# Planner costs, single-engine routing steps, late bias tables and numbered one-hot rows in an attention and expert kernel

## The chip, the cores and the metric

The kernel runs on one core of one Trainium2 chip. The metric is device time in microseconds for one execution; it was taken three times. PE is the matrix engine (TensorE), DVE the vector engine, ACT the scalar engine, POOL is GpSimd, and SP issues most of the DMAs. Each engine executes its own queue in order and waits at an instruction until what that instruction needs is there.

## The reference

Two parts follow each other. Windowed attention for 8 batches and 8 heads over 576 positions with 64 values each (window 128, a linear bias per head), then a layer of 8 experts on the 4608 rows of 512 values. Each token takes the expert with the largest logit, or keeps that of the token before it where a local gate says so.

```python
scores = np.where(mask, scale * q @ k.T + bias, -1e9)   # mask: 0 <= rel < 128
attn = softmax(scores); x = attn @ v                    # rows of 8 heads * 64
for b in range(B):
    for s in range(S):
        fresh_e = argmax(logits[b, s])
        e = fresh_e if s == 0 or local_gate[b, s] < 0.5 else prev_e
        prev_e = e
        p = softmax(logits[b, s])
        out[b, s] = p[e] * (relu(x[b, s] @ w1[e]) @ w2[e])
```

## The kernel before, in words

**Attention** runs over 32 pairs of heads (8 batches of 4 pairs). A pair is a chain of small operations, named by a letter. S (PE) makes nine pieces of scores in PSUM, four banks of them. D (DVE) scales a piece, adds the bias table and takes the row minimum (`scs<-sc`, with a short read of the minimum, `mn`). E (ACT) is the exponential, with its sum; B (DVE) is that sum for two of the pieces, where DVE makes it. A and R (DVE) make the reciprocal of the sums (`r`). P (POOL or DVE) multiplies the piece by it (`cut<-cut,r`). U (PE) transposes (`pt<-ident,cut`), C (ACT or DVE) copies the result out of PSUM (`pts<-pt`), M (PE) multiplies by the values (`xa<-pts,cut`), X (ACT or DVE) copies that out (`xT<-xa`), and T (DVE) transposes 32x32 blocks for the store (`T<-xT`).

The bias tables of a pair are six DVE or POOL operations on `rel` (which lies in the tile `qx`); their results lie in `slopes` and `qx`. Pair 0's six go to DVE; the other 18 may be taken by either engine and wait for nothing.

**Routing** of a batch, `tokens` and `route`, follows when its four pairs are through: logits (PE), then some 35 short steps on DVE and POOL that find the expert of each token, its gate value and its place in that expert's list. `route` gives a one-hot matrix `ro_all` (row within a block) per batch. For the first three experts, which the kernel serves first ("own" visits of 256, 384 and 384 rows), it also builds `cw` and adds the token numbers into a table `tbl`; `early` turns that table into indices, and `gathers` fetches the rows with indirect DMAs on POOL (`kr<-xd,xidx`).

**The planner** (`plan`, `Op`, `steps`) decides the order of all this while the kernel is built: it keeps a clock for each engine, charges every instruction the duration that `cost` gives, and picks the operation that can start first; among equals the smaller due time wins (`DUE`, in pairs). `COPY` and `SHARE` say for each operation which engines may take it, and `SLOWER` is what DVE is charged on top before it takes a copy that ACT could do. A step of a generator in `steps` is one such operation; where a `yield` stands, the next step begins, and its word says on which engine. `BY` is added to the due time from step to step. The instructions of the planned engines keep the planned order; the expert stage behind it is put in between by the framework where it finds room.

**Experts.** `Fixed.run` works through a visit: for each of eight slices of the hidden layer `h<-qx,cut` (PE), relu and a split into two parts (ACT `hh`, DVE `hl`), then `y<-cut,hh`. The weights come in raw (`wraw`) and each half chunk is split by ACT (`CAST cut<-wraw`) and DVE (`TENSOR_TENSOR cut<-wraw,cut`). Rows of a visit are turned by DVE (`xtr<-kr`), ACT (`qx<-xtr`) and DVE (`qx<-xtr,qx`). A tick in between advances `routing`: the routing of batch 7, then `rank_tables` and `fill_table`, which build the lists of the remaining visits from `ro_all` and one-hot columns (`hot`).

## Time and profile before

| what | value |
| --- | --- |
| time, median of 3 (lowest to highest) | 670.52 us (670.30 to 670.69) |
| the profiled execution | 671.84 us, of which the span of the profile is 670.1 us |
| PE busy | 644.6 us (96%) |
| DVE busy | 512.4 us (76%) |
| ACT busy | 412.9 us (62%) |
| POOL busy | 370.6 us (55%) |
| mean granted clock of PE | 0.985 |

Attention ends on PE at about 223.5 us of the span, the experts take the rest. A busy time counts a stretch in which at least one instruction of the engine was under way. A row of the timeline gives start, duration, engine, line, operation, out<-in, shape and count; in brackets stands the idle time of the engine ahead of it and what ended it. Line 226 is the planner's recording helper, so most of attention has this line; the tile names tell the operations apart.

### The profile page before, as it was taken

To read this page: it belongs to the slowest core of one execution; us is meant where nothing else is said; L and a number is where in the kernel's file an instruction comes from. 1 tells how busy PE (TensorE), PEld (TensorE's weight loads), DVE (VectorE), ACT (ScalarE), POOL (GpSimd) and SP (SyncE) were. 2 spreads that over 40 slices of the span, in tenths; PEclk is the share of its full clock that TensorE was granted. 3 is DMA by queue.
4 is the path that set the end of the run, shared out by engine and by line. 5 is a ranking of instruction groups with operands and counts; after the bars stand their busy time and mean duration, and the time that the engine had idled before them with its cause. 6 is when DMAs were issued, how large, how long until landed. Compare 5 with 4: busy or idle time off the path is not lost. (4 is left out here: it accounts for less than half of the span.)

```text
span 670.1 us, 17317 instructions
## 1 busy us (share of the span) xinstructions
PE 644.6 (96%) x5913; PEld 515.0 (77%) x5913; DVE 512.4 (76%) x1882; ACT 412.9 (62%) x1148; POOL 370.6 (55%) x567
## 2 busy tenths in 40 slices
PE   6999999999998989999999999999999999999995
PEld 3676766766665877899888889889988988888663
DVE  7899999999998799896454995675676576566883
ACT  4999999999887563344343554553555455455651
POOL 6456466455856776277651847557476466526411
PEclk7999999999998999999999999999999999999998
DMA  9863965853933674465632576666566574447640
GB/s 284 290 212 120 266 188 150 265 168 114 303 110 108 200 237 159 137 209 159 192 92 95 181 258 181 206 207 203 162 216 207 160 237 118 148 134 226 216 158 21
DMA packets 61964, 122.22 MB, mean 182 GB/s; under 512 B 9687, under 2 KB 28759, under 8 KB 61874
## 3 DMA queue, kind: packets, MB, share of 16 engines
q1 hardware_dynamic: 52322, 101.27, 47.9%
q0 software_dynamic: 9120, 19.24, 9.5%
q8 instruction: 47, 0.77, 0.5%
q10 hardware_dynamic: 432, 0.59, 0.3%
q14 instruction: 43, 0.35, 0.2%
HBM read 102.08 MB, written 19.04 MB: 181 GB/s over the span
## 5 line engine op out<-in xcount | busy, mean ns | idle before, releaser
L242 POOL DMA_INDIRECT kr<-xd,xidx x141 | 158.1, 1122 | 57.8 <-issue 41.6
L312 DVE TENSOR_TENSOR cut<-wraw,cut 128x512 fp32r<-128x512 f32 x232 | 151.4, 687 | 31.1 <-ACT cut L310 30.0
L310 ACT CAST cut<-wraw 128x512 fp32r<-128x512 f32 x222 | 127.0, 618 | 42.1 <-PE y L1333 40.2
L1331 PE MATMUL h<-qx,cut 128*128 128x384 f32 (+7 forms) x408 | 130.4, 320 | 1.7 <-ACT qx L253 1.7
L1332 PE MATMUL h<-qx,cut 128*128 128x384 f32 (+7 forms) x408 | 130.2, 319 | 0.1
L1333 PE MATMUL h<-qx,cut 128*128 128x384 f32 (+7 forms) x408 | 130.2, 319 | 0.0
L226 ACT ACTIVATE cut<-scs,mn 128x192 f32<-128x192 f32 (+2 forms) x288 | 121.1, 436 | 14.4 <-DVE mn L226 13.6
L1331 PE MATMUL y<-cut,hh 128*128 128x512 f32 (+2 forms) x288 | 115.4, 401 | 2.7 <-DVE hh L1421 2.7
L226 POOL TENSOR_SCALAR cut<-cut,r 128x192 f32<-128x192 f32 (+2 forms) x205 | 84.7, 429 | 58.6 <-DVE r L226 17.1
L1318 POOL DMA_INDIRECT out<-y,sidx x41 | 43.9, 1072 | 132.2 <-ACT y L1340 69.6
L1333 PE MATMUL y<-cut,hl 128*128 128x512 f32 (+2 forms) x288 | 114.2, 396 | 0.1
L1332 PE MATMUL y<-cut,hh 128*128 128x512 f32 (+2 forms) x288 | 113.6, 394 | 0.0
L1424 DVE SCALAR_TENSOR_TENSOR hl<-h,hh 128x384 fp32r<-128x384 f32 (+4 forms) x104 | 51.2, 495 | 64.2 <-ACT hh L1423 63.9
L1423 ACT ACTIVATE hh<-h 128x384 fp32r<-128x384 f32 (+4 forms) x98 | 43.7, 446 | 84.5 <-PE h L1333 81.2
L226 PE MATMUL sc<-kr,qx 64*64 64x192 f32 (+2 forms) x1152 | 83.0, 332 | 6.3 <-DVE mn L226 6.3
L1331 PEld LDWEIGHTS h<-qx,cut 128*128 128x128 f32 x408 | 77.4, 190 | 7.4 <-ACT qx L253 2.2
L1332 PEld LDWEIGHTS h<-qx,cut 128*128 128x128 f32 x408 | 77.7, 190 | 5.0 <-DVE qx L255 0.4
L1333 PEld LDWEIGHTS h<-qx,cut 128*128 128x128 f32 x408 | 77.7, 190 | 1.3
L226 PE MATMUL xa<-pts,cut 64*64 64x64 f32 (+1 forms) x1280 | 72.1, 254 | 2.5 <-ACT xT L226 2.2
L1331 PEld LDWEIGHTS y<-cut,hh 128*128 128x128 f32 (+2 forms) x288 | 53.5, 186 | 21.1 <-DVE hl L1424 3.3
L226 PEld LDWEIGHTS xa<-pts,cut 64*64 64x64 f32 (+1 forms) x1280 | 48.1, 135 | 23.9 <-issue 8.7
L226 PE MATMUL pt<-ident,cut 128*128 128x128 f32 x384 | 64.1, 289 | 0.7 <-POOL cut L226 0.7
(237 smaller groups left out, 1043.0 us busy)
## 6 DMA issues: line engine op xcount, KB each, us to landing
wraw<-w SPq DMA_DIRECT2D x120, 512.0 KB
kr<-kT SPq DMA_DIRECT2D x31, 288.0 KB
qx<-qT SPq DMA_DIRECT2D x30, 288.0 KB
cut<-v SPq DMA_DIRECT2D x8, 1024.0 KB
xd<-T SPq DMA_DIRECT2D x8, 640.0 KB
xd<-T SPq DMA_DIRECT2D x8, 512.0 KB
kr<-xd,xidx POOLq DMA_INDIRECT x141, 3.7
v<-v SPq DMA_DIRECT2D x16, 128.0 KB
```

The source lines that it names most:

```text
L226: ins = getattr(self.engine, name)(*args, **kw)
L242: queued(nc.gpsimd.indirect_dma_start(out=r, out_offset=None, in_=src[0:n, :], in_offset=bass.IndirectOffsetOnAxis(ap=col, axis=0), bounds ...
L310: scalar.copy(c[:, 0, f], raw[:, f])
L312: vector.tensor_tensor(c[:, 1, f], raw[:, f], c[:, 0, f], ALU.subtract)
L1318: ins = nc.gpsimd.indirect_dma_start(out=out[:, :], out_offset=bass.IndirectOffsetOnAxis(ap=col, axis=0), in_=y, in_offset=None, bounds_ch ...
L1331: nc.tensor.matmul(o, ah, bh, start=start, stop=False)
L1332: nc.tensor.matmul(o, ah, bl, start=False, stop=False)
L1333: nc.tensor.matmul(o, al, bh, start=False, stop=stop)
L1423: now.act.activation(hh, hp[:, :w], AF.Relu)
L1424: nc.vector.scalar_tensor_tensor(hl, hp[:, :w], 0.0, hh, ALU.max, ALU.subtract)
```

## The change

Seven edits, in one step:

- the planner's durations for some DVE operations are raised, `SLOWER` goes from 34 to 120 and `BY` from 0.113 to 0.172, and `DUE`, `COPY` and `SHARE` hold other values;
- `route` is cut into more steps, each with instructions of one engine; the exponential is issued later, and `rex` is multiplied ahead of `ohs`;
- the 18 tables of pairs 1 to 3 wait each for a D of the pair before;
- `ro_all` is multiplied by the token numbers `val` (POOL; DVE for batch 7), which `hv` did before for `cw`, and `hot` for each column;
- `hot` is one `tensor_tensor` over five columns in place of five `tensor_scalar`;
- `val` already tells three batches apart, so `enter_steps` adds the offset of a batch only from batch 3 on;
- that addition is a POOL step of its own.

```diff
 DUE = {
-    "A0": 0.47, "A1": -0.1,
+    "A0": -1.48, "A1": -2.34,
...
-SCS, SLOWER, SWITCH, STORE, BY = 8, 34, 0, 10000, 0.113
-COPY = {"C0": "aaea", "C1": "aaea", "C2": "aeae", "X0": "eeee", "X1": "aeae"}
-SHARE = ["fpff", "pfpf", "ffff", "fpff", "ffff", "fpff", "ffff", "fffp", "fffp"]
+SCS, SLOWER, SWITCH, STORE, BY = 8, 120, 0, 10000, 0.172
+COPY = {"C0": "aeee", "C1": "aaea", "C2": "aeae", "X0": "eeae", "X1": "aeee"}
+SHARE = ["fppf", "pfpf", "ffff", "fpff", "ffff", "fpfp", "ffff", "fffd", "fffp"]
...
         if name == "tensor_tensor_reduce":
-            return 75 + 1.04 * n
+            return 80 + 1.04 * n
         if name == "tensor_scalar" and 64 <= n <= 192 and args[1].dtype == F32:
-            return 60 + 0.88 * n
+            return 90 + 1.1 * n
+        if name == "tensor_scalar" and n <= 32:
+            return 110
         if name == "tensor_reduce":
-            return 45 + (src if src >= 64 else 1.3 * src)
+            return 66 + 1.05 * src if src >= 64 else 45 + 1.3 * src
...
             dve.tensor_tensor(a5, l8, mb, ALU.is_equal)
+            for _ in step:
+                yield "pool"
             apart.tensor_tensor(a5, a5, kp, ALU.mult)
             apart.tensor_tensor(ex, l8, mb, ALU.subtract)
...
             dve.tensor_reduce(c, a5, AX.X, ALU.max)
-            act.activation(ex, ex, AF.Exp)
...
             dve.tensor_tensor_scan(run_, kT, kT, 0.0, ALU.max, ALU.max)
+            for _ in step:
+                yield "act"
+            act.activation(ex, ex, AF.Exp)
...
+            for _ in step:
+                yield "pool"
+            apart.tensor_tensor(ex, ex, OH, ALU.mult)
             apart.tensor_tensor(ohs, ohs, cn, ALU.add)
-            apart.tensor_tensor(ex, ex, OH, ALU.mult)
...
             dve.tensor_tensor(RO, rep32.unsqueeze(1).broadcast_to([P, NT, P]), rf.unsqueeze(2).broadcast_to([P, NT, P]), ALU.is_equal)
+            for _ in step:
+                yield "pool"
+            apart.tensor_tensor(RO, RO, val[:, b % 3].unsqueeze(2).broadcast_to([P, NT, P]), ALU.mult)
...
-            pool.tensor_tensor(hv, OH[:, :, 0:NS], val[:, 0].unsqueeze(2).broadcast_to([P, NT, NS]), ALU.mult)
-            pool.tensor_tensor(cw, hv.unsqueeze(3).broadcast_to([P, NT, NS, 4 * KS]),
+            yield "pool"
+            pool.tensor_tensor(cw, OH[:, :, 0:NS].unsqueeze(3).broadcast_to([P, NT, NS, 4 * KS]),
                                    kh.unsqueeze(2).broadcast_to([P, NT, NS, 4 * KS]), ALU.mult)
...
+        def enter_steps(table, ps, b):
+            if b < 3:
+                dve.tensor_tensor(table, table, ps, ALU.add)
+                return
+            z = tp.tile([P, P], F32, name="tz")[:, :table.shape[1]]
+            dve.tensor_scalar(z, ps, 0.0, float(S * (b - b % 3)), ALU.is_gt, ALU.mult)
+            dve.tensor_tensor(table, table, ps, ALU.add)
+            yield "pool"
+            pool.tensor_tensor(table, table, z, ALU.add)
...
+            if 0 < n < 4:
+                for j in range(6):
+                    def table(e, j=j):
+                        bias_table(n, j, dve if e == "dve" else pool)
+
+                    tables[n, j] = Op("pool dve", n - 0.9 + 0.1 * j, table, [ops["D", j, n - 1]])
...
-            for t in range(NT):
-                nc.vector.tensor_scalar(fo[b][:, t], io128, fc[:, b * NT + t:b * NT + t + 1], val[:, b % 3, t:t + 1], ALU.is_equal, ALU.mult)
+            nc.vector.tensor_tensor(fo[b], io128.unsqueeze(1).broadcast_to([P, NT, NSB]),
+                                    fc[:, b * NT:b * NT + NT].unsqueeze(2).broadcast_to([P, NT, NSB]), ALU.is_equal)
```

What this does to the order of the instructions is shown at three places; a row is line, operation, out<-in and shape, and xN is a count. Lines of the changed kernel are two higher in the helpers. The first place is DVE's queue at the start, first as it was and then as it is; the rows on `qx` and `slopes` are bias tables, the rows named ISA are D and the reading of its minimum.

```order
L226 TENSOR_SCALAR qx<-qx 64x192 x2
L226 TENSOR_SCALAR slopes<-qx 128x192 x2
L226 TENSOR_SCALAR slopes<-qx 64x192 x2
L226 TENSOR_SCALAR qx<-qx 64x192 x2
L226 TENSOR_SCALAR slopes<-qx 128x192
L226 TENSOR_SCALAR qx<-qx 64x192 x3
L226 TENSOR_SCALAR slopes<-qx 128x192 x2
L226 TENSOR_SCALAR qx<-qx 64x192 x3
L226 ISA scs,mn<-sc,slopes 128x192
L226 ISA mn 128x1
L226 ISA scs,mn<-sc,slopes 128x192
```

```order
L228 TENSOR_SCALAR qx<-qx 64x192 x2
L228 ISA scs,mn<-sc,slopes 128x192
L228 ISA mn 128x1
L228 ISA scs,mn<-sc,slopes 128x192
L228 ISA mn 128x1
L228 ISA scs,mn<-sc,slopes 128x192
L228 ISA mn 128x1
L228 ISA scs,mn<-sc,slopes 128x192
L228 ISA mn 128x1
L228 TENSOR_SCALAR slopes<-qx 64x192
L228 ISA scs,mn<-sc,slopes 128x192
L228 ISA mn 128x1
```

Of the 18 tables of pairs 1 to 3, 15 stood on DVE ahead of the first D; now none does. In all, DVE makes 11 tables in place of 21, and POOL 13 in place of 3.

The second place is POOL's queue at the routing of batch 6, the last one that the planner sees. `ra` and `rex` are steps of it, the DMA rows are gathers of expert rows, and `cut<-cut,r` are P operations.

```order
L242 DMA kr<-xd,xidx_116 128x128
L226 TENSOR_SCALAR cut<-cut,r 128x192
L242 DMA kr<-xd,xidx_116 128x128
L226 TENSOR_SCALAR cut<-cut,r 128x128
L242 DMA kr<-xd,xidx_116 128x128
L226 TENSOR_TENSOR ra<-ra,kp 128x40
L226 TENSOR_TENSOR rex<-L,rm 128x40
L226 TENSOR_SCALAR cut<-cut,r 128x192 x2
L226 TENSOR_SCALAR cut<-cut,r 128x64
```

```order
L228 TENSOR_TENSOR ra<-ra,kp 128x40
L228 TENSOR_TENSOR rex<-L,rm 128x40
L244 DMA kr<-xd,xidx_116 128x128
L228 TENSOR_SCALAR rse<-rse 128x5
L244 DMA kr<-xd,xidx_116 128x128 x2
L228 TENSOR_TENSOR rex<-rex,oh_all 128x40
L228 TENSOR_TENSOR ohs<-ohs,cn 128x8
L228 CAST rrf<-ri 128x5
L228 TENSOR_TENSOR ro_all<-ro_all,val 128x640
L244 DMA kr<-xd,xidx_116 128x128 x9
```

The three gathers ahead of `ra` now stand behind it, no P operation is left behind this routing, and nine further gathers stand behind the multiplication of `ro_all`.

The third place is DVE's queue where attention ends (`T<-xT` is the T operation, and the last of them stands here). The row with 512 columns on `cut<-wraw,cut` is DVE's half of splitting a half chunk of weights; `ed`, `ti` and `bi` belong to `early`, `rc`, `k` and `kT` to the routing of batch 6.

```order
L226 TENSOR_TENSOR ro_all<-rep_91,rrf 128x640
L226 TENSOR_TENSOR cut<-wraw,cut 128x512
L226 STREAM_TRANSPOSE T<-xT 128x10x32
L226 STREAM_TRANSPOSE T<-xT 128x8x32
L226 TENSOR_TENSOR cut<-wraw,cut 128x512
L1424 SCALAR_TENSOR_TENSOR hl<-h,hh 128x256 x2
L312 TENSOR_TENSOR cut<-wraw,cut 128x512
L226 COPY L<-pk 128x36
L226 TENSOR_REDUCE L<-pk 128x9
L312 TENSOR_TENSOR cut<-wraw,cut 128x512
```

```order
L228 TENSOR_REDUCE rc<-ra 128x5
L228 STREAM_TRANSPOSE T<-xT 128x8x32
L228 TENSOR_TENSOR cut<-wraw,cut 128x512
L228 TENSOR_SCALAR ti<-tbl 128x32
L228 TENSOR_SCALAR bi<-ti 128x32
L228 TENSOR_TENSOR k_109<-rc,rf 128x5
L228 SCALAR_TENSOR_TENSOR fi<-bi,ti 128x32
L228 STREAM_TRANSPOSE kT<-k_109 128x32
L228 TENSOR_SCALAR xidx_116<-fi,roff 128x32
L228 SCALAR_TENSOR_TENSOR krun<-kT 128x32
L228 TENSOR_TENSOR cut<-wraw,cut 128x512
L228 TENSOR_TENSOR fi<-tbl,msel 128x32
```

Before, the routing of batch 6 and `early` were done ahead of the last T, and one split stood between it and the first `hl` of an expert. Now 28 short steps of them, the building of `ro_all` for batch 6 and six splits stand behind the last T and ahead of the copy of batch 7's logits. On PE, 22 products of the first visit (`h<-qx,xT`) stood among the last products of attention; now all of them stand behind it. The first five loads of raw weights, which stood on SP behind the stores of batch 5, now stand among the loads of batch 2.

## Rows read from the trace of the kernel before

**Rows 1.** busy time by stretch; the first line names the columns.

```profile
core 0: us, PE busy (x) PEld busy (x) DVE busy (x) ACT busy (x) POOL busy (x), PEclk, DMA share, GB/s
7.80:18.10 10.30, 7.40 (x64) 4.92 (x65) 8.40 (x53) 7.21 (x28) 4.70 (x26) 0.50 1.07 330
20.00:200.00 180.00, 176.19 (x3089) 123.22 (x3087) 170.65 (x1027) 166.64 (x601) 100.04 (x269) 1.00 0.64 195
205.80:209.20 3.40, 3.27 (x24) 2.04 (x24) 3.29 (x14) 2.83 (x11) 1.89 (x4) 0.50 0.20 76
225.00:250.00 25.00, 22.96 (x141) 19.32 (x141) 24.36 (x79) 15.60 (x34) 18.80 (x16) 1.00 0.79 245
250.00:640.00 390.00, 388.48 (x2134) 333.89 (x2134) 266.32 (x574) 191.92 (x398) 217.79 (x196) 1.00 0.57 179
```

**Rows 2.** timeline of DVE and PE, 3 to 13 us.

```profile
3.22 1.22 DVE L226 TENSOR_SCALAR slopes<-qx 128x192 f32<-128x192 f32 x4 [2.21 <-POOL qx L226]
9.22 0.36 DVE L226 CUSTOM_DVE_ANT_0 scs<-sc,slopes 128x192 f32<-128x192 f32 x1
4.54 1.19 PE L226 MATMUL sc<-kr,qx 64*64 64x192 f32 x18
10.01 1.99 PE L226 MATMUL sc<-kr,qx 64*64 64x192 f32 x20 [4.28 <-DVE mn L226]
```

**Rows 3.** groups by shape, 0:225 us; busy us, mean ns, then idle us

```profile
L226 DVE COPY xT<-xa 128x320 f32<-128x320 f32 x7 | 3.4, 482 | 0.2 <-PE xa L226 0.2
L226 DVE TENSOR_SCALAR cut<-cut,r 128x192 f32<-128x192 f32 x59 | 21.1, 380 | 0.3
L226 DVE TENSOR_SCALAR qx<-qx 64x192 f32<-64x192 f32 x10 | 2.7, 280 | 0.1
L226 ACT COPY pts<-pt 128x512 f32<-128x512 f32 x93 | 54.3, 583 | 7.4 <-PE pt L226 6.6
L226 POOL TENSOR_SCALAR cut<-cut,r 128x192 f32<-128x192 f32 x165 | 70.7, 442 | 57.0 <-DVE r L226 15.6 <-DVE mn L226 13.3 <-ACT pts L226 6.0
L226 POOL TENSOR_SCALAR qx<-qx 64x192 f32<-64x192 f32 x2 | 1.8, 881 | 0.1
L226 POOL TENSOR_TENSOR cw<-hv,kh 128x240 f16<-128x240 f16 x6 | 3.5, 589 | 4.1 <-DVE kh L226 4.1
```

**Rows 4.** timeline of POOL, ACT and PE around 205 us.

```profile
203.74 1.10 POOL L242 DMA_INDIRECT kr<-xd,xidx  x1 [0.17 <-issue]
205.38 0.24 ACT L226 ACTIVATE rex<-rex 128x40 f32<-128x40 f32 x1 [1.59 <-POOL rex L226]
205.93 0.91 PE L226 MATMUL xa<-pts,cut 128*64 128x128 f32 x6 [2.17 <-ACT xT L226]
```

**Rows 5.** timeline of PE, DVE and ACT, 222 to 249 us.

```profile
222.07 0.28 PE L1333 MATMUL h<-qx,xT 128*128 128x256 f32 x1
222.88 0.28 PE L1331 MATMUL h<-qx,xT 128*128 128x256 f32 x1
224.05 0.84 DVE L226 STREAM_TRANSPOSE T<-xT 128x320 f32<-128x320 f32 x2 [2.06 <-ACT xT L226]
227.67 0.19 DVE L226 TENSOR_REDUCE rm<-L 128x5 f32<-128x40 f32 x1
229.19 0.17 DVE L226 TENSOR_REDUCE rse<-rex 128x5 f32<-128x40 f32 x1
246.79 0.70 DVE L249 STREAM_TRANSPOSE xtr<-kr 128x512 f32<-128x512 f32 x1
247.63 0.61 ACT L253 CAST qx<-xtr 128x512 fp32r<-128x512 f32 x1
248.29 0.62 PE L1331 MATMUL h<-qx,cut 128*128 128x384 f32 x2 [1.75 <-ACT qx L253]
```

**Rows 6.** groups by shape of DVE, 225 to 670 us.

```profile
L1196 DVE TENSOR_SCALAR cw<-io,at_t,val 128x128 f16<-128x128 f16 x80 | 20.3, 330 | 0.7 <-PE tr L1211 0.6
L226 DVE TENSOR_TENSOR ro_all<-rep,rrf 128x640 f16<-128x640 f16 x1 | 0.8, 781 | 0.0
```

More of the change, by code (lines that the diff above doesn't have):

```diff
@@ L761, in route @@
             pe.matmul(ends, run_[:, 31:32].broadcast_to([P, P]), perm, start=True, stop=True)
+            for _ in step:
+                yield
             dve.tensor_reduce(se, ex, AX.X, ALU.add)
-            apart.tensor_scalar(se, se, 1e-9, 1.0, ALU.add, ALU.mult)
+            if not step:
+                apart.tensor_scalar(se, se, 1e-9, 1.0, ALU.add, ALU.mult)
             yield from gap()
@@ L770, in route @@
             for _ in step:
+                yield "pool"
+                apart.tensor_scalar(se, se, 1e-9, 1.0, ALU.add, ALU.mult)
                 yield
@@ L794, in route @@
             dve.reciprocal(se, se)
+            for _ in step:
+                yield "pool"
+            apart.tensor_tensor(ex, ex, OH, ALU.mult)
             apart.tensor_tensor(ohs, ohs, cn, ALU.add)
-            apart.tensor_tensor(ex, ex, OH, ALU.mult)
             yield from gap()
@@ L812, in route @@
             dve.tensor_scalar(ri, ri, 31, None, ALU.bitwise_and)
+            for _ in step:
+                yield "pool"
             apart.tensor_copy(rf, ri)
@@ L828, in route @@
             dve.tensor_tensor(RO, rep32.unsqueeze(1).broadcast_to([P, NT, P]), rf.unsqueeze(2).broadcast_to([P, NT, P]), ALU.is_equal)
+            for _ in step:
+                yield "pool"
+            apart.tensor_tensor(RO, RO, val[:, b % 3].unsqueeze(2).broadcast_to([P, NT, P]), ALU.mult)
             if b >= EARLY[-1][1]:
@@ L844, in route, with enter @@
             yield
-            enter(tbl, pT, b, pool)
+            yield from enter_steps(tbl, pT, b)
             routed.append(b)
             yield "free"
-        def enter(table, ps, b, apart=None):
+        def enter_steps(table, ps, b):
[5 more added lines that the diff above has]
+            dve.tensor_tensor(table, table, ps, ALU.add)
+            yield "pool"
+            pool.tensor_tensor(table, table, z, ALU.add)
+        def enter(table, ps, b):
             if b == 0:
@@ L856, in enter @@
             dve.tensor_tensor(table, table, ps, ALU.add)
-            (apart or dve).tensor_tensor(table, table, z, ALU.add)
+            dve.tensor_tensor(table, table, z, ALU.add)
         def indices(t, idx, x0, c0, visits):
@@ L1132, in moe_attention @@
         tables = {}
-        for p in range(1, 4):
-            for j in range(6):
-                def table(e, p=p, j=j):
-                    bias_table(p, j, dve if e == "dve" else pool)
-                tables[p, j] = Op("pool dve", p - 0.9 + 0.1 * j, table)
         ops["set"] = mark()
```

6 lines of the change are left out of this document (4 added, 2 removed), and 22 rows, old and new, of the table DUE.

## The prediction, made before the changed kernel ran

> **What bounds the kernel now.** I read the busy times by stretch first, then the timeline at the places where PE has a gap, then the groups by shape for prices. Between 20 and 200 us PE is busy 176.19 of 180 us at full clock, DVE 170.65, ACT 166.64, POOL 100.04 [rows 1]. PE sets the pace of attention, and DVE and ACT stand close behind it; only POOL has room. From 250 to 640 us PE is busy 388.48 of 390 us and DVE only 266.32 [rows 1], so nothing that DVE saves there moves the end. What the change can move is therefore PE's idle time and its half clock in the first 250 us, in four places: the start, the middle, the routing of batch 6 and the handover to the experts.
>
> **The start.** DVE begins to make tables at 3.22 and makes 21 of them before the first D at 9.22. PE ran its first 18 score products from 4.54 to 5.73 and then stood still for 4.28 us until a D had freed a bank of PSUM [rows 2]. In the changed order DVE makes pair 0's six tables and goes to D: four at 1.22 us together and two `qx` tables at 0.28 [rows 2, 3] end at about 5.0. D then waits for scores alone, until about 5.9 in place of 9.22. **Term: -3.3 us.** PE's gap shrinks to about 1 us, and what is late next is D itself, one piece after another, then ACT's exponentials, which follow D in order. The 18 tables are not gone: ten more of them go to POOL. There they cost 4.4 us at the price of a P of the same width (442 ns) or 8.8 us at that of a table made while DVE makes its own (881 ns) [rows 3]. DVE will not be making tables, so I take the first; POOL's room of 80 us in 180 hides it [rows 1]. Without that cover a P behind a table would come 0.4 to 0.9 us late.
>
> From 7.8 to 18.1 us PE's granted clock is 0.50, that is 1.2 GHz, after the 4.28 us in which it did nothing; it is busy 7.40 us of that stretch [rows 1, 2], and 3.7 us of these are the price of the half clock. With the gap gone the clock may stay up. But at full clock PE will wait for ACT's exponentials there, and gaps may bring it down again. Bounds: 0 to -3.7 us; I take a quarter, as the row shows only that the low clock follows a long gap. **Term: -0.9.**
>
> **The middle.** Counting the built order, DVE loses 5 PSUM copies (482 ns for the wider X), 6 P operations net (380), 10 tables (280) and two additions, some 8 us in all; ACT gains the 5 copies, at most 5 x 583 ns = 2.9 us [rows 3]. The due times and shares bring the rest. A faster DVE does not speed PE up where PE never waits. It can return the 3.81 us that PE is idle there [rows 1]; I take a quarter, **-1.0**, with 0 to -3.8 as bounds. ACT, busy 92.6% of this stretch, may make PE wait where it did not; between 0 and +2.9 I take **+0.7**, since its 13.4 us of idle time hide most of the copies.
>
> POOL gets seven multiplications of `ro_all` with 640 elements. The nearest row is `cw` with 240 elements, 589 ns [rows 3]: 0.59 us if size cost nothing, 1.57 us if all of it went with size. I take 1.3 us, so 9 us for seven, less the `hv` step that falls away. POOL's free time hides it, and the planner knows its price; without that cover the P operations queued behind each one, and the transposes on PE behind them, would come up to 1.57 us late (second rival).
>
> **The routing of batch 6.** A gather started on POOL at 203.74 and held the two routing steps behind it; ACT waited 1.59 us for `rex` at 205.38, and the X copy behind it on ACT came so late that PE stood still for 2.17 us [rows 4]. Right behind it the granted clock is 0.50 with PE busy 3.27 of 3.40 us [rows 1], which costs 1.6 more. In the new order the two steps stand ahead of the gathers, the exponential stands three steps later, and PE has finished attention by then: this wait has nobody left to hold up. **Term: -3.8** (bounds 0 and -3.8).
>
> **The handover.** This is where the change costs. From 225 to 250 us DVE is busy 24.36 of 25 us [rows 1]: it, not PE, sets when the second visit starts. Its last T began at 224.05, it reached the third `xtr` at 246.79, ACT cast it at 247.63, and PE began at 248.29 after a gap of 1.75 us [rows 5]. In the new order the following stands between the same two instructions of DVE in addition: 28 short steps at (229.19 - 227.67)/9 = 0.17 us from start to start [rows 5], 4.7 us; `ro_all` of batch 6 and its multiplication for batch 7, 0.78 each [rows 6]; one split more (512 columns, for which I take the 0.70 us of the `xtr` of 512 columns beside it [rows 5]); one `hl` of 256 columns less (half of that, -0.35). Sum: 4.7 + 1.6 + 0.7 - 0.35 = +6.6 us. PE has more to do there as well: the 22 products of the first visit that used to fill attention, at (222.88 - 222.07)/7 = 0.116 us each [rows 5], 2.6 us, and 0.6 us of batch 6's routing products. Moving these 3.2 us costs nothing by itself, since attention is shorter by as much. What is left is DVE's excess, 6.6 - 3.2: PE's gap of 1.75 grows to about 5.1. **Term: +3.4** (0 if DVE catches up because it loses work, +6.6 if PE's extra work does not overlap).
>
> **The one-hot columns.** 80 `tensor_scalar` at 330 ns (20.3 us busy) become 16 `tensor_tensor` of the size that took 781 ns [rows 6], 12.5 us. All lie where PE is the bound, so 0 on the path; without that cover it would still be a gain. Weight loads that stand earlier on SP meet no reader that waits: 0.
>
> **Sum against the profiled execution:** -3.3 - 0.9 - 1.0 + 0.7 - 3.8 + 3.4 = -4.9 us, from 671.84 to 666.9. The median of the three runs, 670.52, lies 1.32 below that execution, so the forecast is 665.6 us.
>
> **A rule weighed.** A table on POOL took 881 ns while DVE made tables, a P of the same width 442 when mostly other work ran [rows 3]; something that both engines use was taken. The Trainium skill, "SBUF — State Buffer", section "SBUF: two separate sides", says that DVE and GpSimd share one pair of ports, held for a whole instruction, with the other engine blocked. The rows agree with it as far as they go. By that rule the seven long multiplications could hold DVE, which is the second rival.
>
> **Rivals.**
> 1. *The clock stays up at the start and most of PE's idle time in the middle returns.* For it: low clock follows long gaps in both rows that show it, and DVE gets 8 us freer. Against: ACT's chain of exponentials paces the first pairs. It gives the other 2.8 us of clock and 2.8 us of idle time: 660.0.
> 2. *POOL's multiplications hold DVE and the P operations.* At most 7 x 1.57 = 11 us of holding; DVE has 9.4 us of idle time in the middle, which hides more than half, so about +4.3 is left: 669.9, no difference that can be told. Against: 442 against 881 ns shows POOL losing, not DVE.
> 3. *The second visit waits for its rows: slower.* Its last nine gathers stand on POOL behind the `ro_all` multiplication of batch 6. By the sum DVE builds that `ro_all` some 10 us after the last T; add 1.3 for the multiplication and nine gathers of 1.27 us (1.10 and the 0.17 ahead of it [rows 4]), 11.4, and they are issued after 23 us, while DVE reaches the third `xtr` after 28.5. That leaves 5 us. The routing changes engines some ten times, and if it loses 1.3 us each time, as ACT and PE lost 1.59 and 2.17 at one such place [rows 4], the gathers come 13 us late and PE waits 8 us more: 673.6. It decides from the point where `ro_all` is built later than about 15 us behind the last T.
> 4. *The early D does not advance the start*, because the next matrices have not landed or POOL's tables are late for pair 1. Then -0.9 and two thirds of -3.3 are missing: 668.7.
>
> **How the numbers follow.** Forecast 55% (663 to 668.5), rival 1 17%, rival 2 12%, rival 3 11%, rival 4 5%. About 0.2%, 1.3 us, is what a measurement of this kernel can tell from no change. Faster: 55 + 17 + 5 = 77%; same: 12%; slower: 11%. The range from 660.5 to 671.2 leaves out rival 3 and about half of rival 1.
>
> **What would show it.** Right: the first D near 5.9 and PE's gap after its first scores near 1 us; no 2 us gap on PE with ACT's `rex` ahead of it; attention's last product on PE near 212 us in place of 223.5, and the second visit's first product near 243.4 in place of 248.29, with a gap of about 5 us ahead of it; from there the same distance to the end. Wrong: new gaps of PE on `pt` or `xa` between 20 and 200 us (ACT or POOL has become the bound); DVE's P or T rows longer beside POOL's multiplications; gathers as the releaser of the third `xtr`; a granted clock of 0.50 where it is 1.00 now.

## The result, and the profile after

| | before | after |
| --- | --- | --- |
| median (lowest to highest) | 670.61 us (670.27 to 671.74), 6 runs | 679.55 us (678.17 to 682.60), 6 runs |
| profiled execution, its span | 671.84, 670.1 us | 678.80, 677.1 us |

The ratio is 1.0139, with a 95% interval of 1.0117 to 1.0160: slower by 9 us, where 665.6 had been forecast and 671.2 was the upper end. The two profiled executions lie 7.0 us apart, and the bookkeeping below is made on these.

The same view of busy time by stretch as in [rows 1], now of the changed kernel, with one stretch in place of another where the low clock has moved:

```profile
core 0: us, PE busy (x) PEld busy (x) DVE busy (x) ACT busy (x) POOL busy (x), PEclk, DMA share, GB/s
7.80:18.10 10.30, 7.14 (x58) 4.30 (x57) 7.01 (x42) 6.21 (x23) 9.50 (x22) 0.67 1.06 331
20.00:200.00 180.00, 174.84 (x3065) 120.60 (x3064) 160.31 (x983) 167.39 (x604) 105.26 (x279) 0.99 0.62 193
72.70:76.20 3.50, 3.50 (x32) 1.93 (x26) 1.66 (x10) 2.76 (x10) 0.00 (x0) 0.51 0.49 139
216.10:219.50 3.40, 3.40 (x52) 2.66 (x52) 0.03 (x1) 0.64 (x2) 0.28 (x1) 0.50 0.00 0
225.00:250.00 25.00, 21.06 (x153) 16.91 (x153) 22.19 (x85) 9.95 (x24) 19.08 (x20) 0.93 0.66 205
250.00:640.00 390.00, 386.31 (x2129) 335.00 (x2131) 263.53 (x516) 194.33 (x399) 233.16 (x205) 1.00 0.58 183
```

DVE did lose work, 10 us of it between 20 and 200 us (170.65 to 160.31), as the change was read to do. In all PE did not gain: it is idle 5.2 us there where it was idle 3.8, but 3.1 of the 5.2 are one stall on SP, shown below. Between 225 and 250 us it is idle 3.9 us where it was 2.0. The row of 216.1 shows PE alone at work, at half clock, with DVE at 0.03 us of 3.40, just ahead of the stretch in which the prediction had DVE as the bound.

**The start.** Timeline of DVE, PE and POOL, 5 to 14 us, which answers to [rows 2]:

```profile
5.50 0.36 DVE L228 CUSTOM_DVE_ANT_0 scs<-sc,slopes 128x192 f32<-128x192 f32 x1 [0.58 <-PE sc L228]
6.29 1.10 PE L228 MATMUL sc<-kr,qx 64*64 64x192 f32 x20 [0.54 <-DVE mn L228]
8.86 0.95 POOL L228 TENSOR_SCALAR qx<-qx 64x192 f32<-64x192 f32 x1
10.18 1.24 POOL L228 TENSOR_SCALAR cut<-cut,r 128x192 f32<-128x192 f32 x3
11.48 0.90 PE L228 MATMUL pt<-ident,cut 128*128 128x128 f32 x3 [1.93 <-POOL cut L228]
12.47 0.85 POOL L228 TENSOR_SCALAR slopes<-qx 128x192 f32<-128x192 f32 x1
13.70 0.36 DVE L228 CUSTOM_DVE_ANT_0 scs<-sc,slopes 128x192 f32<-128x192 f32 x1 [1.69 <-PE sc L228]
```

The first D comes at 5.50 (forecast 5.9), and the gap of 4.28 us has become one of 0.54. But then the transposes wait 1.93 us for P operations that stand on POOL behind tables. The gaps of PE in the first 24 us are 4.97 us before (4.28 and 0.69) and 4.40 after (0.54, 0.29, 0.70, 1.93, 0.54, 0.40). The groups by shape of POOL, 0 to 225 us, say what a table costs there, for [rows 3]:

```profile
L228 POOL TENSOR_TENSOR ro_all<-ro_all,val 128x640 f16<-128x640 f16 x6 | 7.9, 1317 | 3.3 <-DVE ro_all L228 3.3
L228 POOL TENSOR_SCALAR qx<-qx 64x192 f32<-64x192 f32 x7 | 6.2, 890 | 0.5
L228 POOL TENSOR_SCALAR slopes<-qx 128x192 f32<-128x192 f32 x5 | 4.4, 880 | 0.3
```

**A stall on SP.** Timeline of SP and PE, 63 to 73 us; a row of SP is the issuing of DMAs, and L675 is a no-op of SP on which PE waits between two groups of `xa` products:

```profile
63.61 0.38 SPq L414 DMA_DIRECT2D cut<-v  x1
65.31 2.85 SPq L694 DMA_DIRECT2D xd<-T  x2
68.25 3.83 SPq L843 DMA_DIRECT2D gd<-gT  x4
68.45 0.66 PE L228 MATMUL pt<-ident,cut 128*128 128x128 f32 x4
72.19 0.34 PE L228 MATMUL xa<-pts,cut 64*64 64x64 f32 x8 [3.08 <-SPq L675]
```

The four stores of gate values took 3.83 us to issue; the no-op stood behind them, and PE behind the no-op. Their input `gT` was ready at 67.2. It was the first of the four that took long, 2.66 us from 68.25 on, behind the V loads (`cut<-v` of 1 MB and two smaller ones) and two large stores `xd<-T`; the other three took 0.45, 0.29 and 0.28. The same line over the whole run, 32 stores, with shortest, median and longest time in ns:

```profile
L843 SPq DMA_DIRECT2D gd<-gT x32: 271/288/2657, 68.2 to 247.9; - x32
```

What held the first one so long is not shown. Before, the same four stores were issued ahead of the V load:

```profile
60.52 1.32 SPq L826 DMA_DIRECT2D gd<-gT  x4
66.23 0.40 SPq L412 DMA_DIRECT2D cut<-v  x1
```

PE's clock is at half for 3.4 us right behind this gap (row of 72.70 above).

**The handover.** Timeline of PE, ACT and DVE, 217 to 252 us, for [rows 4, 5]:

```profile
217.23 2.15 PE L228 MATMUL pk<-xT,w 128*32 128x128 f32 x40
219.44 0.32 ACT L228 COPY part<-pk 128x192 f32<-128x192 f32 x1 [2.57 <-PE pk L228]
219.66 0.62 ACT L228 CAST xT<-wraw 128x512 fp32r<-128x512 f32 x1
220.31 0.69 DVE L228 TENSOR_TENSOR xT<-wraw,xT 128x512 fp32r<-128x512 f32 x1 [4.18 <-ACT xT L228]
225.35 0.37 PE L228 MATMUL pk<-perm,krun 128*128 128x20 f32 x2 [1.16 <-DVE krun L228]
228.45 0.50 PE L1363 MATMUL y<-cut,hl 128*128 128x512 f32 x1 [1.67 <-DVE hl L1454]
248.22 0.50 PE L1361 MATMUL y<-cut,hh 128*128 128x512 f32 x1 [1.23 <-ACT hh L228]
250.49 1.22 PE L1363 MATMUL y<-cut,hl 128*128 128x512 f32 x2 [1.07 <-DVE hl L1454]
```

The logits of batch 6 (40 products, `pk<-xT,w`) came at 217.23, before at 197.52. ACT's copy of them (`part`) stood in ACT's queue ahead of a weight cast, and DVE, whose next instruction was its half of that split, stood idle for 4.18 us, immediately ahead of the stretch in which it has the most to do. The split goes into a tile of `xT` that these logits read, so it has to wait for them as well.

### The profile page after: what moved, and what is told of

Its sections match the earlier page's. It is cut to its first block, busy times and chain, and to the rows that moved or that the text cites. A ratio compares the mean times of both kernels' runs of the same rounds, so it can differ in the third digit from the quotient of the medians.

```text
span 677.1 us, 17261 instructions
## 1 busy us (share of the span) xinstructions
PE 645.9 (95%) x5913; PEld 515.1 (76%) x5913; DVE 500.3 (74%) x1796; ACT 415.2 (61%) x1153; POOL 392.0 (58%) x582
## 5 line engine op out<-in xcount | busy, mean ns | idle before, releaser
L244 POOL DMA_INDIRECT kr<-xd,xidx x141 | 161.2, 1143 | 45.9 <-issue 41.1
L1348 POOL DMA_INDIRECT out<-y,sidx x41 | 46.0, 1121 | 132.8 <-ACT y L1370 69.9
L228 PE MATMUL sc<-kr,qx 64*64 64x192 f32 (+2 forms) x1152 | 79.0, 330 | 0.8 <-DVE mn L228 0.8
L228 PE MATMUL xa<-pts,cut 64*64 64x64 f32 (+1 forms) x1280 | 70.3, 254 | 4.7 <-SPq L675 3.7
L228 PEld LDWEIGHTS xa<-pts,cut 64*64 64x64 f32 (+1 forms) x1280 | 47.3, 135 | 29.6 <-issue 12.6
```

The lines of the kernel that those rows point to most:

```text
L228: ins = getattr(self.engine, name)(*args, **kw)
L244: queued(nc.gpsimd.indirect_dma_start(out=r, out_offset=None, in_=src[0:n, :], in_offset=bass.IndirectOffsetOnAxis(ap=col, axis=0), bounds ...
L1348: ins = nc.gpsimd.indirect_dma_start(out=out[:, :], out_offset=bass.IndirectOffsetOnAxis(ap=col, axis=0), in_=y, in_offset=None, bounds_ch ...
```

## The experiments

Two kinds of number are compared: the median with its ratio to the kernel before on the same chip, and places in the trace. The last column but two is the third visit's first product on PE; from there to PE's last product it is 373.7 to 374.0 us in every trace from e5 on, before and after too, so it carries the difference between two profiled executions, up to 0.7 us. "Distance" is from attention's last product to the second visit's first (in e13, six products of the first visit, 1.4 us, stand behind that point).

| kernel | first D | pair 2's first D | logits of batch 6 | attention's last product | distance | third visit | median, us | ratio to before (95%) |
| --- | --- | --- | --- | --- | --- | --- | --- | --- |
| before | 9.22 | 20.18 | 197.5 | 223.6 | 24.7 | 288.4 | 670.6 | 1 |
| after | 5.50 | 19.02 | 217.2 | 221.0 | 35.2 | 295.1 | 679.6 | 1.0139 (1.0117 to 1.0160) |
| e5, gate stores behind | 5.39 | 19.36 | 212.8 | 216.8 | 35.1 | 290.6 | 675.5 | 1.0084 (1.0063 to 1.0104) |
| e6, old steps | 5.99 | 19.26 | 204.7 | 229.5 | 25.7 | 292.0 | 675.9 | 1.0106 (1.0068 to 1.0143) |
| e7, before + late tables | 5.53 | 17.86 | 204.1 | 228.8 | 24.7 | 292.0 | 674.8 | 1.0066 (1.0043 to 1.0090) |
| e8, before + numbers in rows | 9.21 | 20.01 | 204.1 | 230.1 | 25.7 | 294.1 | 678.5 | 1.0112 (1.0077 to 1.0147) |
| e9, before, rex on DVE | 9.25 | 19.66 | 197.2 | 222.4 | 24.7 | 285.6 | 671.8 | 1.0017 (0.9989 to 1.0045) |
| e10, e5 + tables first | 8.90 | 18.39 | 211.8 | 216.4 | 34.3 | 288.1 | 674.7 | 1.0048 (1.0034 to 1.0062) |
| e11, before + planner's numbers | 8.90 | 20.34 | 204.1 | 226.6 | 25.1 | 290.3 | 673.5 | 1.0039 (1.0024 to 1.0053) |
| e12, before + finer steps | 9.25 | 20.38 | 207.4 | 226.6 | 25.2 | 290.3 | 674.4 | 1.0058 (1.0037 to 1.0080) |
| e13, before, gathers later | 9.24 | 20.06 | 197.7 | 221.5 | 22.4 | 288.5 | 669.3 | 0.9992 (0.9978 to 1.0005) |
| e14, e9 and e13 | 9.25 | 20.01 | 197.7 | 222.8 | 21.9 | 286.2 | 670.1 | 1.0005 (0.9989 to 1.0021) |
| e15, e5 + tables on DVE | 6.20 | 16.40 | 215.7 | 219.4 | 35.1 | 293.3 | 675.4 | 1.0071 (1.0044 to 1.0098) |
| e16, e5 + old one-hot form | 6.20 | 19.36 | 212.6 | 216.4 | 35.2 | 291.3 | 674.8 | 1.0075 (1.0046 to 1.0103) |
| e17, e5 + logits free | 6.20 | 18.19 | 190.6 | 215.9 | 31.9 | 285.2 | 669.3 | 0.9983 (0.9967 to 0.9999) |
| e18, e10 + logits free | 8.90 | 20.36 | 193.0 | 216.9 | 32.8 | 287.0 | 671.0 | 1.0003 (0.9982 to 1.0024) |

The four kernels e1 to e4 ran on a chip on which every kernel, that of before too (762 us), was longer by 60 to 90 us, with pauses of several engines at once from about 235 us on. There e1 to e4 came out at 0.966, 1.009, 0.980 and 0.983 of before; no total of theirs is used, only their first 200 us.

Places at the start have to be read with care. e5 and e17 have the same order on DVE, ACT and POOL up to 190 us, and so have e10 and e18; yet pair 2's first D came at 19.36 and 18.19 us in the first two, at 18.39 and 20.36 in the other two. A microsecond or two there is no difference between kernels.

### The gate stores (e1 and e5)

```diff
-            for a in range(4):                      # stores of gd, in the middle of route
+            def store_gates():
+                for a in range(4): ...
...
             yield from enter_steps(tbl, pT, b)
+            store_gates()
             routed.append(b)
```

On SP this moves nothing but PE's no-op, which in three batches now stands ahead of the four stores; the order on DVE, ACT and POOL is unchanged.

> The changed kernel, with the four stores of gate values of a batch issued at the end of its routing instead of in its middle; on SP the no-op that PE waits for then stands ahead of them. Theory A: the 3.08 us gap of PE at 69 us, and the 3.4 us of half clock behind it, come from that no-op waiting on SP behind the four stores, the last of which waits for the V load to land. Without it 679.55 - 3.1 - 1.7 = 674.8 us, and no gap over 0.5 us there. Rival: the wait only moves on to the next instruction that needs the V load or to DVE's backlog; then the gap shrinks but the time stays at 678 or above.

> The same kernel as e1_gates_behind, on another chip: there every kernel of that call lost some 80 us to pauses of several engines at once in the expert stage, the kernel before too, so that only its first 200 us could be read. There the gap at 69 us was gone and the last product of attention came at 216.8 in place of 221.0 us. Theory A: 679.55 - 4.2 = 675.3 us, ratio to before 1.007. Rival: what is gained is waited for at the handover, 678 or above.

Measured in e5: 675.49 us, as theory A had it. (That the last store waits for the V load, as e1's theory has it, cost nothing: in the changed kernel it was issued 0.06 us behind the third. The first store was the long one.) SP and PE there:

```profile
69.42 3.19 SPq L845 DMA_DIRECT2D gd<-gT  x4
69.15 0.66 PE L228 MATMUL pt<-ident,cut 128*128 128x128 f32 x4
69.74 0.34 PE L228 MATMUL xa<-pts,cut 64*64 64x64 f32 x8
```

The stores still take 3.19 us to issue, but PE goes on without a gap, and there is no half clock behind it. Attention's last product moves from 221.0 to 216.8. So 4.1 of the 9 us (3.7 by the ratios, as e5 ran on another chip) are this one no-op's place in SP's queue.

### BY small (e2), and the routing cut as before (e3 and e6)

```diff
-SCS, SLOWER, SWITCH, STORE, BY = 8, 120, 0, 10000, 0.172
+SCS, SLOWER, SWITCH, STORE, BY = 8, 120, 0, 10000, 0.09
```

e3 and e6 take from the changed kernel the new `yield`s of `route` up to the rounding step, and the new places of the exponential and of `rex`; BY stays at 0.172.

> The changed kernel with BY = 0.09 in place of 0.172 and nothing else. Theory A: the routing was cut into about twice as many steps and BY is charged for each, so that its due times run past the end of attention; with the small BY the routing of batch 6 ends ahead of the last T again, and the gate stores of batch 1 stand ahead of the V load. Then the handover costs no more than before (about 8.5 - 1.75 = 6.8 us back) and the stall at 69 us goes (4.8 us): 679.55 - 11.6 = 668 us, 666 to 670. Rival B: the finer steps and the long POOL multiplications cost engine time by themselves, wherever they stand: 676 or above.

> The changed kernel with the routing cut as before (old steps, old places of the exponential and of rex), all other edits and all new numbers kept, BY = 0.172 too. Theory A (steps times BY is the cause, neither is alone): the routing of batch 6 stands ahead of the last T; 667 to 671 us. Rival B (the long POOL multiplications of ro_all, which stay): 676 or above. Rival C (the planner's other numbers spoil the middle): 673 to 677, with PE's gaps between 20 and 200 us.

> The same kernel as e3_no_new_steps (changed kernel with the routing cut as before), on another chip. Theory A (the number of steps times BY puts the routing of batch 6 behind attention, and that costs the handover 8.5 us): 668 to 671 us. Rival (the routing ahead of the last T costs as much there, by waits of PE on the routing and on the rows of the first visit between 185 and 225 us, as in the trace of before and of e2): 675 or above, with the second visit's first products near 256 us as in the changed kernel.

Measured in e6: 675.91 us, the rival. The routing of batch 6 stands ahead of the last T again, and the distance from attention to the second visit is 25.7 us, as before. But attention ends at 229.5: what the handover gives back, the end of attention takes. The stall at 69 us is gone in this order too (one of 1.52 us at 95 us is new), so the kernel to compare with is e5 (675.49): no difference. e2 shows the same at 200 us, where PE waits for the routing, DVE for a cast of ACT and ACT for PE's transposes:

```profile
198.64 0.69 DVE L257 TENSOR_TENSOR qx<-xtr,qx 128x512 fp32r<-128x512 f32 x1 [1.90 <-ACT qx L255]
200.12 0.19 PE L228 MATMUL pk<-oh_all,utri 128*128 128x40 f16 x1 [2.70 <-DVE oh_all L228]
```

So theory A of e3 and e6, that the routing of batch 6 should simply stand where it stood, falls: by its place alone nothing is won.

### Each group of edits alone (e7, e8, e11, e12)

The kernel before with one group of hunks: the late tables (e7), the token numbers in the one-hot rows (e8), `DUE` to `SHARE` and `cost` (e11), the finer steps (e12).

> The kernel before with the late bias tables alone (the tables of pairs 1 to 3 wait for a D of the pair before; nothing else). Theory A from the traces of e1 and e4: the first D comes 3.5 us earlier, but pair 2's first D no earlier, since ten tables on POOL stand ahead of P operations and PE waits for those; 0 +- 1.3 us against before, 669.3 to 671.9. Rival, the step of the prediction: -3.3 us for the early D and up to -3.7 for the clock, 663.5 to 667.3.

> The kernel before with the token numbers in the one-hot rows alone (ro_all times val on POOL, hot in one operation, the addition for a batch as a step of its own). Theory A: seven POOL multiplications of 1.26 us are hidden and the hot operations stand where PE is the bound: within 1.3 us of before, 669.3 to 671.9. Rival B: the hot operations of 128x640 hold DVE for 0.8 us in one piece and delay the split and hl behind them, as the gap of 1.06 us on PE with cw ahead of it at 262 us of the changed kernel suggests, and POOL's multiplications delay P: +1 to +3 us.

> The kernel before with the planner's new numbers alone (durations, DUE, SLOWER, BY, COPY, SHARE). Routing 6 stays ahead of the last T in the built order. Theory A (any new order of attention meets waits that the planner does not see, 180 to 225 us above all, as in e6, e7 and e8): 674 to 678 us. Rival (durations nearer to the traced ones give a better order; the loss of the change comes from the steps): 664 to 669.

> The kernel before with the finer steps of the routing alone (old numbers, BY 0.113). Theory A (as for e11): 674 to 678 us, with attention's last product near 229 us and 25 us from there to the second visit. Rival (finer steps keep an engine from waiting in the middle of a step): 666 to 670.

All four are slower than before, by 0.66, 1.12, 0.39 and 0.58%, or 4.4, 7.5, 2.6 and 3.9 us; e7 and e8 lie outside both ranges that had been expected. In e7 pair 2's first D comes at 17.86 us, where five executions of the old order at the start have 19.66 to 20.18, a hint that the start gained; the loss comes later. In e8 pair 24's first D is at 155.4 us (154.9 before), so the multiplications on POOL cost at most 0.5 us up to there; at attention's last product it is 6.5 us late, with this as its largest gap:

```profile
189.20 0.69 PE L226 MATMUL pt<-ident,cut 128*128 128x128 f32 x2 [3.47 <-DVE g L226]
```

In all four the loss is of that kind: other gaps of PE at 180 to 222 us, where routing, gathers and the first visit's rows run beside the last pairs, with 6.8 to 10.2 us of half clock there in e7, e8 and e11 (3.4 in before), and in e7 also gaps of 1.0 to 1.3 us at 25, 88 and 136 us. That the due times of before fit the operations of before, and those of after the operations of after, would explain it; which wait of each kernel does it was not taken apart, so that stays open.

### The stall at batch 6's routing (e9, e13, e14)

```diff
+            near = dve if b == NB - 2 else apart              # e9, e14
-            apart.tensor_tensor(a5, a5, kp, ALU.mult)
-            apart.tensor_tensor(ex, l8, mb, ALU.subtract)
+            near.tensor_tensor(a5, a5, kp, ALU.mult)
+            near.tensor_tensor(ex, l8, mb, ALU.subtract)
...
-SOONER = 3                                                    # e13, e14
+SOONER = 0
```

> The kernel before with two short steps of batch 6's routing (the product for ra and the difference rex, 0.27 us each) on DVE in place of POOL; the order is the same up to about 200 us. It takes away what the exponential waited for at 205 us (POOL behind a gather) and leaves the routing where it stands. Theory A, the prediction's step: PE's gap of 2.18 us and the 3.4 us of half clock behind it go, -3.8: 666.7 us. Rival: DVE is at 97 to 98% there, so that the wait comes back as waits for P, T or xtr before the second visit: 669 to 671.

> The kernel before with the three gathers for the second visit that stand among the last P operations on POOL moved behind attention (SOONER 0 in place of 3); the order is the same up to about 200 us. Theory A: the gap of 2.18 us of PE at 203.8 us in before, and of 2.40 us at the same place in e9 where ACT no longer waited for rex, comes from the gather on POOL, which holds whatever stands behind it (rex, then P). Without it no gap over 1 us between 195 and 215 us, no half clock behind it, 670.5 - 2.2 - 1.6 = 666.7 us. Rival: three gathers of 1.27 us each then stand ahead of the second visit's rows and it begins 2 to 4 us later relative to attention's end, or another wait takes the place: 669.5 to 672.

> The kernel before with both edits, rex and ra of batch 6 on DVE (e9) and the three gathers behind attention (e13). Theory A: as e13, and DVE no longer waits for POOL's ra at 205 us: 665.5 to 667. Rival: 669.5 to 672.

Measured: 671.75, 669.32 and 670.11 us, none apart from before. In e9 ACT waits 0.21 us for `rex` in place of 1.59 [rows 4], and PE still stands still at the same place:

```profile
203.36 1.10 POOL L242 DMA_INDIRECT kr<-xd,xidx  x1 [0.17 <-PE sc L226]
203.63 0.24 ACT L226 ACTIVATE rex<-rex 128x40 f32<-128x40 f32 x1 [0.21 <-DVE rex L226]
206.14 0.44 PE L226 MATMUL pt<-ident,cut 128*128 128x128 f32 x2 [2.40 <-POOL cut L226]
```

Behind the gather of 1.10 us on POOL now a P is late in place of `rex`. With the gathers moved (e13) the gap goes (0.38 us is left of it), and attention ends 2.1 us earlier, yet the median moves by 0.7. The profiled execution of e13 was the slowest of its twelve (671.96 us); there the rest is given back behind the second visit's start, where the one-hot columns are late for PE and the clock is at half for 6.8 us (3.4 in before), after a stretch in which DVE was busy 21.66 of 22.40 us:

```profile
206.07 0.55 PE L226 MATMUL pt<-ident,cut 128*128 128x128 f32 x3 [0.38 <-POOL cut L226]
252.05 1.17 PE L1211 MATMUL tr<-cw,ro_all 128*128 128x128 f16 x5 [1.04 <-DVE cw L1196]
221.50:243.90 22.40, 21.42 (x170) 18.49 (x170) 21.66 (x73) 13.18 (x30) 17.71 (x16) 1.00 0.67 216
```

### The tables (e4, e10, e15)

e4 and e10 let the tables of pairs 1 to 3 go from the start, in the changed kernel (e10 with the gate stores behind). e15 keeps them late, on DVE alone:

```diff
-                    tables[n, j] = Op("pool dve", n - 0.9 + 0.1 * j, table, [ops["D", j, n - 1]])
+                    tables[n, j] = Op("dve", n - 0.9 + 0.1 * j, table, [ops["D", j, n - 1]])
```

> The changed kernel with the tables of pairs 1 to 3 free from the start again, as before; all else as changed. Theory A: the late tables are worth what PE's gaps and clock in the first 23 us show between the two traces, (4.97 - 4.40) of gaps and 1.7 of half clock, 2.3 us: 679.55 + 2.3 = 681.9 us, with the first D near 9 us again. Rival: the ten tables on POOL delay the P operations of pair 0 (gap of 1.93 us at 9.5 us) by as much as the early D gains: 678 to 680, no difference.

> The changed kernel with the gate stores at the end of the routing (as e1 and e5) and the tables of pairs 1 to 3 free from the start, as before. Theory A (late tables only move the wait to P behind tables on POOL: pair 2's first D came at 19.4 us with late tables in e5 and at 18.4 with early ones in e4): 675.5 - 0.9 = 674.6 us. Rival, the prediction's step: 675.5 + 2 to 4 = 677.5 to 679.5.

> The kernel of e5 (changed, gate stores behind) with the 18 late tables made by DVE alone. Theory A (P operations of the first pairs stand behind tables on POOL): the gap of 1.93 us at 9.4 us with POOL's cut ahead of it falls below 0.5 us and pair 2's first D comes before 18.4 us in place of 19.4; the rest of attention pays for 13 tables more on DVE with other P shares, so that the time may stay at 674 to 677. Rival (D waits for tables whichever engine makes them, and DVE is the scarce one there): pair 2's first D at 19.4 us or later.

Measured: e10 674.72 us, theory A's 674.6, with 1.0048 of before against 1.0084 in e5. But the same pair with the logits freed, e17 (late tables) and e18 (tables from the start) below, lies the other way round, 0.9983 and 1.0003. So no gain of 2 to 4 us by the late tables is seen, and whether they gain or lose anything in the changed kernel stays open. In e15 pair 2's first D comes at 16.40, earlier than in any other run, and no transposes wait there for POOL:

```profile
9.35 1.49 PE L228 MATMUL sc<-kr,qx 64*64 64x192 f32 x14 [0.51 <-DVE mn L228]
10.81 1.12 PE L228 MATMUL pt<-ident,cut 128*128 128x128 f32 x4
7.80:18.10 10.30, 9.44 (x92) 5.68 (x92) 9.76 (x60) 9.23 (x35) 6.59 (x25) 0.83 1.03 294
```

So it is the tables on POOL, with P behind them, that made the gap of 1.93 us after the early D. Not all of the 3.0 us from e5 is this gap: the clock was at half for 3.4 us there, and for 10.2 in e5. The time is 675.42 nevertheless, the same as e5: pair 10 is already 1.7 us later than in e5 (67.2 and 65.4). DVE has 13 tables more; that these are the reason was not tested.

### The one-hot columns (e16)

```diff
-            nc.vector.tensor_tensor(fo[b], io128..., fc..., ALU.is_equal)
+            for t in range(NT):
+                nc.vector.tensor_scalar(fo[b][:, t], io128, fc[:, b * NT + t:b * NT + t + 1], 1.0, ALU.is_equal, ALU.mult)
```

> The kernel of e5 with each one-hot row block made by five tensor_scalar operations of 128 columns again (equality alone, the token numbers stay in ro_all). Theory A, the prediction's step: DVE has 8 us more to do in the expert stage, none of it on the path: within 1.3 us of 675.5. Rival: the one operation of 0.8 us holds hl and the split, and the gaps of 0.97 and 0.63 us at 258 to 260 us go: 673 to 674.2. Other rival: DVE's 8 us count: 677 to 680.

Measured: 674.75 us, 0.7 from e5: the form of these operations is off the path, as predicted.

### The late logits (e17 and e18)

```diff
-steps("pe", n + DUE["tokens"], 0.1, side(), xs + [ops["set"]] + prior, mark=ops["read", b], small=1)
+steps("pe", n + DUE["tokens"], 0.1, side(), xs + [ops["set"]] + (prior if b < NB - 2 else []), mark=ops["read", b], small=1)
```

`prior` is the end of the routing of the batch before; only the last planned batch loses it.

> The kernel of e5 (changed, gate stores behind) in which the logits of batch 6 no longer wait in the plan for the routing of batch 5. Theory A: each routing now ends late in the next batch, so that the logits of batch 6 came at 212.8 us (217.2 in the changed kernel, 197.5 before); ACT's copy of them stood ahead of the weight cast, and DVE, which is the bound of the handover, was idle for 3.95 us at 212 us (4.18 in the changed kernel) behind that cast. With the logits free this idle time goes, and 17 products of the first visit fill attention's gaps again: third visit's first product 290.6 - 4 = 286.6 us, time 671.5, 670 to 673. Rival: what DVE gains it waits for later (rows of the second visit, POOL), 674.5 to 676.5.

> The kernel of e10 (changed, gate stores behind, tables of pairs 1 to 3 free from the start) with the logits of batch 6 freed as in e17. Theory A: 674.7 - 4 = 670.7 us, no difference from before. Rival: as for e17, 673.5 to 675.5.

Measured: e17 669.33 us, 6.2 less than e5 and the only version here whose interval lies below before, by 0.17%, and it ends at 0.9999; e18 670.96, 3.8 less than e10. e17 gained more than had been expected, e18 as much. PE and DVE of e17, and its busy time where [rows 1] has 22.96 and 24.36:

```profile
190.56 1.19 PE L228 MATMUL pk<-xT,w 128*32 128x128 f32 x40
208.54 0.64 DVE L228 TENSOR_TENSOR xT<-wraw,xT 128x512 fp32r<-128x512 f32 x1
210.00 0.68 DVE L228 TENSOR_TENSOR xT<-wraw,xT 128x512 fp32r<-128x512 f32 x1
225.00:250.00 25.00, 22.06 (x137) 18.84 (x136) 23.00 (x77) 14.12 (x30) 19.51 (x19) 1.00 0.60 190
```

The logits come 22 us earlier than in e5, the two splits into `xT` follow without a wait of DVE, and from 225 to 250 us the clock stays at 1.00, where it was 0.86 in e5 and 0.93 in the changed kernel. The distance to the second visit falls from 35.1 to 31.9 us and attention ends 0.8 us earlier. The account by DVE's idle time fits e5 but not e10: there the logits are as late (211.8 us), yet DVE has no idle time over 1.9 us between 195 and 256 us, and freeing them still gave 3.8 us. What held e10 was not taken apart.

## Why the prediction was wrong, step by step

From before to after, in the profiled executions: the change in PE's gaps (those of over 0.12 us) and in the clock's price (half of PE's busy time in the stretches at half clock).

| step of the prediction | predicted | measured | of which gaps, clock |
| --- | --- | --- | --- |
| start, with its clock | -4.2 | -1.2 | -0.6, -0.6 |
| weight loads and SP's queue | 0 | +4.8 | +3.1, +1.7 |
| middle (idle time, ACT's copies) | -0.3 | -3.1 | -3.1, 0 |
| batch 6's routing, end of attention | -3.8 | +0.9 | +0.8, +0.1 |
| handover, up to the third visit | +3.4 | +6.5 | +4.9, +1.6 |
| sum | -4.9 | +7.9 | +5.1, +2.7 |

The third visit's first product itself is 6.7 us later. The sum is 1.2 over that; that some of the work at half clock would have waited for other engines at full clock too may be the reason, but it is not shown.

**SP's queue: the step that failed outright.** The prediction looked at SP for the weight loads alone and gave them 0. The four gate stores had moved as well, behind the V load and the `xd` stores, with PE's no-op behind them. It cost 4.8 us in the trace, and 4.1 between the medians or 0.55% (3.7 us) between the ratios (e5). The row to look at was in the order, not in the trace: a wait of PE that runs through another queue takes on whatever is put ahead of it there.

**The start.** The mechanism of the early D was right (first D at 5.50, gap of 0.54), and ten tables on POOL were taken at 442 ns with 881 as the other bound. They cost 880 to 890 ns, also at 12.47 us while DVE stood idle (no DVE row between 12.01 and 13.70). The cover that was named, POOL's 80 us of room in 180, does not exist in the first 20 us, where POOL is busy 9.50 of 10.30 us. The step named its own loss, "a P behind a table would come 0.4 to 0.9 us late", and left it out of the sum; three P operations behind tables made 1.93. The clock's part cannot be told from chance, given the spread at the start between executions of one order; and the half clock of before had set in inside the gap of 4.28 us, not behind it [rows 1, 2].

**The rule weighed.** The port that DVE and GpSimd share ("SBUF — State Buffer", section "SBUF: two separate sides", in the Trainium skill) had been matched to 881 against 442 ns. With DVE idle and the table still at 0.85 us, that reading falls. A table multiplies and takes a maximum, both with constants; a P multiplies twice, once by a column; so the instruction itself differs, and which part of it makes the factor of two was not tested. The long multiplications on POOL took 1.32 us (1.3 predicted), and here the blocking that the rule speaks of does show, in the direction of the second rival:

```profile
211.70 1.63 POOL L228 TENSOR_TENSOR ro_all<-ro_all,val 128x640 f16<-128x640 f16 x1 [0.80 <-DVE ro_all L228]
212.51 0.84 DVE L228 TENSOR_SCALAR r<-sm 128x5 f32<-128x5 f32 x1
213.99 0.33 PE L228 MATMUL pt<-ident,cut 128*128 128x128 f32 x1 [0.57 <-DVE cut L228]
```

The A operation on DVE (`r<-sm`), 0.17 us in the median of 64, took 0.84 and ended with the multiplication; the P and the transposes behind it were late, and PE stood still for 0.57 us. In e17 a `qx<-xtr,qx` of 512 columns took 1.52 us beside such a multiplication (0.69 in the median), with a gap of 1.05 us on PE behind it. The rival had a true cost, then, of one gap of PE and not of 4.3 us.

**The middle** gained 3.1 of the 3.8 us of idle time, where a quarter had been taken; rival 1 was nearer there. Which of the edits returned it was not taken apart.

**Batch 6's routing.** The gap of 2.17 us went with its place, but the cause was named too narrowly: not `rex`, but the gather ahead of it on POOL (e9). And the time fell on other operations: nine gaps of 0.1 to 0.6 us, 3.6 us in all, and a stretch at half clock. The routing of batch 5 now stood where that of batch 6 had been; only for the gap of 0.57 us above is a holder seen.

**The handover.** DVE's way from the last T to the third `xtr` took 29.6 us (223.27 to 252.89), with 1.75 us of waiting for ACT in it, and the prediction's sum gives 29.3; the gaps of PE up to the second visit come to 5.13 us, and 5.1 had been forecast. But the 5.13 are four gaps inside the first visit (1.16, 1.67, 1.23, 1.07), and the second visit's first product at 256.23 follows PE's own work without a gap: that the two numbers meet is in part luck. Three things were missed. DVE was idle 4.18 us ahead of its busiest stretch, behind the late logits. The clock fell twice behind such gaps (229.8 and 250.2 us, at 0.50), once more than before, where it had fallen at 250.2 only. And behind the second visit's start, where the prediction had assumed the same distance to the end, a one-hot column was late for PE (1.05 us) and an `hl` behind the next (0.63 us). Freeing the logits gave 6.2 us in e17 and 3.8 in e18.

**Rival 3**, slower by way of the second visit, had the right side with the wrong mechanism: in the changed kernel no `xtr` of the second visit waited for a gather (in e10, e17 and e18 one does, 1.2 to 2.3 us). Its 673.6 was 6 us short.

The two causes that the runs showed, the no-op's place on SP (4.1 us) and the logits behind the routing of batch 5 (3.8 to 6.2 us), make up 7.9 to 10.3 of the 9 us. With both mended the seven edits stand 0.17% below before (e17) or level with it (e18, tables from the start); the first, one of fourteen versions, is at the edge of what these runs can tell. The forecast had been 0.7% below.

## What to carry to other kernels

When a planner's order is changed, follow each small operation that moved on every queue, the ones that only issue DMAs too, and ask who waits for a no-op, a copy or a store behind it: the two that decided here (four stores of 0.6 KB, one copy of 192 columns) hardly show in a list of busy time. A stall that is removed has to be traced to what holds the queue, not to the instruction that was seen waiting; as long as the holder stands there, the next instruction behind it is late. And a group of edits made for each other is not a sum of gains: each group of this change alone cost 2.6 to 7.5 us, perhaps because due times fit the operations that they were made for.

## What the runs showed of the hardware

- A `tensor_scalar` on POOL with a multiplication and a maximum took 880 to 890 ns for 192 columns, with 64 or 128 partitions alike; with two multiplications 445 ns.
- The length of the stretch at half clock at the start is not fixed by the order. It was 10.2 us in the trace of before and 6.8 in e9, whose order on DVE, ACT and POOL is the same for 200 us, and 10.2 us in e5 and 3.4 in e17, the same for 190. Pair 2's first D came 0.5 and 1.2 us apart in these two pairs, and 2.0 us apart in e10 and e18.
- Four stores of 0.5 to 0.6 KB took 1.32 us to issue on SP ahead of a load of 1 MB and 3.83 behind it and two stores of 0.5 and 0.6 MB; of the 3.83, the first store alone took 2.66, where the median of 32 is 0.29.
- A `tensor_scalar` of 4 or 5 columns on DVE took 0.72 to 0.85 us beside POOL's `tensor_tensor` of 640 columns (0.17 without; four times in e8, once in the changed kernel), each time until that instruction's end. D, reductions and transposes on DVE kept their times beside it (D of 192 columns 0.35 us either way). And the multiplication itself took 1.63 us in place of 1.25 where a `tensor_tensor` of 512 columns was under way on DVE when it began.
